# The order of three loads of a unit: first half of K, V, second half of K becomes first half, second half, V

## The chip, the cores and the metric

The kernel runs on one core of a Trainium2 chip. The metric is the device time of one execution in microseconds (us). The times quoted are medians. Single runs of the same kernel lie within about 0.5% of their median for the kernel before. A run counts as slow when it is over 1.5% above the fastest run of the same kernel; only fast runs are compared, and where a slow one plays a part the text says so.

## The reference, cut to what matters

```python
B, Sq, D = 8, 32, 1024
Hq, Hkv, Sk, Dh = 32, 4, 8192, 128
W = min(4096, max(256, Sk // 4))               # 2048
rep = Hq // Hkv                                # 8
q = (x @ wq).reshape(B, Sq, Hq, Dh).transpose(0, 2, 1, 3)
k = repeat(k_cache[:, :, Sk - W:, :], rep, axis=1)
v = repeat(v_cache[:, :, Sk - W:, :], rep, axis=1)
scores = einsum("bhqd,bhkd->bhqk", q, k) * Dh ** -0.5
o = einsum("bhqk,bhkd->bhqd", softmax(scores), v)
return o.transpose(0, 2, 1, 3).reshape(B, Sq, Hq * Dh) @ wo
```

All is bf16. A pair of batch and K/V head is called a **unit**. There are 8 x 4 = 32 units, and each has 2048 rows of K and of V, 512 KB each.

## The kernel before

TensorE makes the scores of a unit (128 keys by 256 queries at a time), ScalarE takes their exponential, and TensorE multiplies the result with V. For the scores, K has to be turned, and there are three ways of it: units 0, 1 and 2 (`PE_T`) are turned by TensorE, eleven units (`V_T`: 4, 7, 9, 12, 14, 17, 19, 22, 24, 27, 29) by VectorE and GpSimd, and the other 18 are turned by the load itself, in two halves of 256 KB. This text calls those halves **a** and **b**. All loads of this phase are issued by one engine, SyncE, one after the other, in program order.

```python
def load_k(self, ui, part=None):
    ...                                         # V_T and PE_T: a plain load into k_raw
    else:
        H = KT // 2
        nc.sync.dma_start_transpose(out=self.kT[ui][:, part * H:(part + 1) * H, :],
                                    in_=src.rearrange("(p j) d -> p (j d)", j=KT)[:, part * H * P:(part + 1) * H * P])

def load_v(self, ui, eng):
    self.v_sb[ui] = self.vp.tile([self.P, self.KT, self.Dh], BF16, name="v_sb", tag="v")
    n = self.KT // (2 if ui >= V_HALVES else 1)
    for j in range(0, self.KT, n):
        eng.dma_start(out=self.v_sb[ui][:, j:j + n, :], in_=...)      # 512 KB, packets of 4096 bytes

def load_unit(self, ui):
    if ui < len(self.units):
        if ui not in V_T:
            self.load_k(ui, None if ui in PE_T else 0)
        self.load_v(ui, self.nc.sync)
        if ui not in V_T and ui not in PE_T:
            self.load_k(ui, 1)
    ...                                         # then plain loads: k_raw of a later unit, pieces of wq and wo

def va_copy(self, ui):                          # V into a padded tile, by VectorE
    out, in_ = self.va[ui % 3][:, :, 0:self.Dh], self.v_sb[ui][:, :, :]
    ...

# in the main loop: 4 slots a unit; the loads of unit u are issued at slot 4 * (u - 5)
loads = {8: [4, 5, 6, 7], **{4 * (u - 5): [u] for u in range(8, len(self.units))}}
```

## Time and profile before

| | kernel before |
|---|---|
| time, median of 3 runs | 183.69 us (183.51 to 184.1) |
| span of the profiled execution | 182.0 us |
| TensorE busy | 98% |
| last load of K, V or weights has landed | 164.0 us |
| bytes moved | 51.72 MB |
| a 512 KB V load, from issue to landing (median) | 7.0 us |
| stretches over 0.3 us in which TensorE does nothing, after 4.5 us | none |

How to read it: TensorE never waits, so it sets the time. But the DMA engines are busy until 164 us as well, and the loads run only a little ahead of TensorE.

### The profile page before, as it was taken

To read this page: it belongs to the slowest core of one execution; us is meant where nothing else is said; L and a number is where in the kernel's file an instruction comes from. 1 tells how busy PE (TensorE), PEld (TensorE's weight loads), DVE (VectorE), ACT (ScalarE), POOL (GpSimd) and SP (SyncE) were. 2 spreads that over 40 slices of the span, in tenths; PEclk is the share of its full clock that TensorE was granted. 3 is DMA by queue.
4 is the path that set the end of the run, shared out by engine and by line. 5 is a ranking of instruction groups with operands and counts; after the bars stand their busy time and mean duration, and the time that the engine had idled before them with its cause. 6 is when DMAs were issued, how large, how long until landed. Compare 5 with 4: busy or idle time off the path is not lost.

```text
span 182.0 us, 5032 instructions
## 1 busy us (share of the span) xinstructions
PE 178.3 (98%) x2041; PEld 152.7 (84%) x2041; DVE 125.3 (69%) x256; ACT 136.3 (75%) x147; POOL 89.5 (49%) x139
## 2 busy tenths in 40 slices
PE   7999999999999999999999999999999999999994
PEld 2999999999999999988787899988787788888853
DVE  0228897699977687679599765697478997354253
ACT  2218898897897888997878787887877788888800
POOL 2004691399918749449686097395078396000000
PEclk9999999999999999999999999999999999999999
DMA  4999999999999999999999999999999999990003
GB/s 177 385 407 405 258 386 321 197 351 195 318 391 251 356 275 325 351 315 362 247 395 257 374 388 249 360 308 286 387 254 286 344 248 388 231 214 0 0 32 91
DMA packets 52953, 51.72 MB, mean 284 GB/s; under 512 B 39744, under 2 KB 40256, under 8 KB 52928
## 3 DMA queue, kind: packets, MB, share of 16 engines
q1 hardware_dynamic: 52352, 50.90, 99.0%
q10 hardware_dynamic: 576, 0.49, 0.8%
q8 instruction: 15, 0.25, 0.5%
q14 instruction: 10, 0.08, 0.1%
HBM read 41.42 MB, written 0.52 MB: 230 GB/s over the span
## 4 chain that ended last, share of the span: by engine, by line
PE 96%; DMA 2%; DVE 0%; issue 0%
PE o_ps L517 32%; PE s_ps L506 31%; PE op_ps L321 15%; PE q_ps L284 12%; PE q_ps L404 3%; DMA x_sb<-in_x_dram 2%; PE xT_ps L380 1%; PE ql_ps L300 1%; PE tp L244 1%; PE kf_ps L396 0%; DVE o_t L331 0%; PE cnt_ps L572 0%
## 5 line engine op out<-in xcount | busy, mean ns | idle before, releaser
L508 ACT ACTIVATE pT<-s_ps 128x1024 bf16<-128x1024 f32 x128 | 128.4, 1027 | 26.7 <-PE s_ps L506 26.4
L269 POOL TENSOR_SCALAR kTv<-kb 32x512 bf16<-32x512 bf16 x127 | 84.7, 667 | 48.8 <-DVE kb L259 27.3
L517 PE MATMUL o_ps<-va,pT 128*128 128x129 bf16 x1024 | 78.8, 220 | 0.0
L517 PEld LDWEIGHTS <-pT 128*128 128x128 bf16 x1024 | 68.5, 98 | 3.2
L506 PE MATMUL s_ps<-QT,kT 128*128 128x256 bf16 x336 | 50.2, 272 | 0.0
L506 PEld LDWEIGHTS <-kT 128*128 128x128 bf16 x336 | 31.9, 98 | 9.4
L321 PE MATMUL op_ps<-wo_sb,OT 128*128 128x512 bf16 (+2 forms) x144 | 36.0, 355 | 0.0
L438 DVE COPY va<-v_sb 128x2048 bf16<-128x2048 bf16 x30 | 25.4, 847 | 7.5 <-DMA v_sb<-in_v_cache_dram 7.1
L259 DVE STREAM_TRANSPOSE kb<-k_raw 128x512 bf16<-128x512 bf16 x44 | 29.5, 687 | 0.6 <-DMA k_raw<-in_k_cache_dram 0.3
L284 PE MATMUL q_ps<-xT,wq_sb 128*128 128x256 bf16 x192 | 28.3, 273 | 0.0
L506 PE MATMUL s_ps<-QT,kTv 128*128 128x256 bf16 x176 | 26.4, 272 | 0.0
L267 DVE COPY kTv<-kb 32x512 bf16<-32x512 bf16 x49 | 22.4, 456 | 1.2
L506 PEld LDWEIGHTS <-kTv 128*128 128x128 bf16 x176 | 17.0, 98 | 6.1
L444 DVE RECIPROCAL RL_all<-o_ps 128x2 f32<-128x2 f32 x32 | 5.3, 165 | 23.6 <-PE o_ps L517 23.3
L284 PEld LDWEIGHTS <-wq_sb 128*128 128x128 bf16 x192 | 16.9, 98 | 1.1
L450 DVE STREAM_TRANSPOSE OT<-o_sb 128x256 bf16<-128x256 bf16 x32 | 14.3, 445 | 1.1
L448 DVE TENSOR_TENSOR o_sb<-o_ps,RL_all 128x256 bf16<-128x256 f32 x32 | 13.6, 424 | 1.1
L321 PEld LDWEIGHTS <-OT 128*128 128x128 bf16 x144 | 11.4, 98 | 2.3 <-DVE OT L450 0.2
L436 POOL TENSOR_SCALAR va<-v_sb 128x2048 bf16<-128x2048 bf16 x2 | 3.8, 1897 | 14.2 <-DMA v_sb<-in_v_cache_dram 14.1
L287 ACT CAST QT<-q_ps 128x512 bf16<-128x512 f32 x12 | 7.0, 583 | 0.2 <-PE q_ps L284 0.2
L328 DVE TENSOR_TENSOR oacc<-op_ps,oacc 128x512 f32<-128x512 f32 x8 | 5.3, 662 | 2.5 <-PE op_ps L321 2.5
L404 PE MATMUL q_ps<-xT,wq_sb 128*128 128x256 bf16 (+1 forms) x64 | 6.0, 246 | 0.0
(35 smaller groups left out, 44.8 us busy)
## 6 DMA issues: line engine op xcount, KB each, us to landing
v_sb<-in_v_cache_dram SPq DMA_DIRECT2D x30, 512.0 KB, 7.0
wo_sb<-in_wo_dram SPq DMA_DIRECT2D x16, 512.0 KB, 6.7
wq_sb<-in_wq_dram SPq DMA_DIRECT2D x13, 512.0 KB, 6.6
k_raw<-in_k_cache_dram SPq DMA_DIRECT2D x13, 512.0 KB, 5.9
wq_sb<-in_wq_dram SPq DMA_DIRECT2D x6, 256.0 KB, 4.8
v_sb<-in_v_cache_dram SPq DMA_DIRECT2D x4, 256.0 KB, 5.1
kT<-in_k_cache_dram SPq DMA_TRANSPOSE x36, 7.3
k_raw<-in_k_cache_dram SPq DMA_DIRECT2D x2, 256.0 KB, 6.2
```

The source lines that it names most:

```text
L259: nc.vector.transpose(out=st["kb"][:, :, sl], in_=self.k_raw[ui][:, :, sl])
L267: nc.vector.tensor_copy(out=out, in_=in_)
L269: nc.gpsimd.tensor_scalar(out=out, in0=in_, scalar1=1.0, scalar2=1.0, op0=ALU.mult, op1=ALU.mult)
L284: nc.tensor.matmul(st[k][:, hl % 2, :], lhsT=self.wq_t[g, i][:, c % (DC // 2), hl * P:(hl + 1) * P], rhs=self.xT[:, c, :], start=(c == 0 a ...
L321: nc.tensor.matmul(ps[:, 0:w], lhsT=self.OT[:, gq, c, t * P:(t + 1) * P], rhs=self.wo_t[gq][:, c, n0:n0 + w], start=(k == 0), stop=(k == 7))
L404: nc.tensor.matmul(ps, lhsT=self.wq_t[0, c // H][:, c % H, h * P:(h + 1) * P], rhs=self.xT[:, c, 0:n], start=(c == 0 and h in (0, 2, 4)), ...
L438: self.nc.vector.tensor_copy(out=out, in_=in_)
L448: nc.vector.tensor_tensor(out=o_sb[:, :, :, :], in0=o_ps[:, :, 0:Dh].rearrange("p q (i c) -> p q c i", c=4), in1=rl[:, ui * QT_N:(ui + 1) ...
L450: nc.vector.transpose(out=self.OT[:, g * QT_N:(g + 1) * QT_N, :, b * self.Sq:(b + 1) * self.Sq], in_=o_sb[:, :, :, :])
L506: nc.tensor.matmul(s_ps[:, jj, :], lhsT=self.kT[ui][:, c * CJ + jj, :], rhs=q_u, start=True, stop=True)
L508: nc.scalar.activation(out=pT[:, :, :], in_=s_ps[:, :, :], func=ACT.Exp, bias=0.0, scale=self.scale)
L517: nc.tensor.matmul(o_ps[:, qt, 0:self.VW], lhsT=pT[:, jj, qt * P:(qt + 1) * P], rhs=va[:, j, 0:self.VW], start=(j == 0 and qt == 0), stop= ...
```

## The change

Its intent is to have the whole of K there earlier. V is needed later than K, so it is put behind both halves.

```diff
         if ui < len(self.units):
             if ui not in V_T:
                 self.load_k(ui, None if ui in PE_T else 0)
+                if ui not in PE_T:
+                    self.load_k(ui, 1)
             self.load_v(ui, self.nc.sync)
-            if ui not in V_T and ui not in PE_T:
-                self.load_k(ui, 1)
```

In 18 units the order a, V, b becomes a, b, V. The programs of TensorE, VectorE, ScalarE and GpSimd are the same, instruction by instruction; only SyncE's order differs.

## The prediction

> **What bounds the kernel now.** I read the page of the profile first: part 1 (busy shares), part 2 (slices), part 4 (the chain that ended last).
>
> ```profile
> PE 178.3 (98%) x2041; PEld 152.7 (84%) x2041; DVE 125.3 (69%) x256; ACT 136.3 (75%) x147; POOL 89.5 (49%) x139
> PE   7999999999999999999999999999999999999994
> DMA  4999999999999999999999999999999999990003
> PE 96%; DMA 2%; DVE 0%; issue 0%
> ```
>
> TensorE is busy for 178.3 of 182.0 us, and the chain is TensorE in 96% of the span; its only long DMA piece is the load of x at the start. The next view is the list of waits, for TensorE alone and then for VectorE:
>
> ```profile
> PE warm_ps L372 <- PEq L680: 0.8, 1, 0.8
> PE xT_ps L380 <- DMA x_sb<-in_x_dram: 0.2, 1, 0.2
> ...
> DVE RL_all L444 <- PE o_ps L517: 23.3, 20, 3.2
> DVE va L438 <- DMA v_sb<-in_v_cache_dram: 7.1, 8, 1.9
> ```
>
> The first two lines are all that TensorE ever waits for over 0.15 us. From the starts of single matmuls in the trace: after 4.5 us no two follow each other by more than 0.3 us. So TensorE never waits for a K or a V now. The last line is the only place where a load of the kind that is moved stops an engine: VectorE stands 7.1 us in all before the copy of V into the padded tile.
>
> But the slices show a second resource that is full: the DMA engines are busy in 9 or more tenths until slice 36, about 164 us. Whether the loads arrive in time is therefore a matter of a microsecond. I lined up the landing of each load with the first instruction that needs it. Unit 11 is the tightest:
>
> ```profile
> 58.96 1.42 SPq L200 DMA_TRANSPOSE kT<-in_k_cache_dram  x1
> 60.48 0.52 SPq L208 DMA_DIRECT2D v_sb<-in_v_cache_dram  x1
> 61.05 1.61 SPq L200 DMA_TRANSPOSE kT<-in_k_cache_dram  x1
> ...
> 65.58 0.60 PE L506 MATMUL s_ps<-QT,kT 128*128 128x256 bf16 x4
> 66.31 0.69 DVE L438 COPY va<-v_sb 128x2048 bf16<-128x2048 bf16 x1
> 68.23 0.56 PE L517 MATMUL o_ps<-va,pT 128*128 128x129 bf16 x7
> ```
>
> The columns are start and duration. The first half of K, V and the second half of K land at 65.14, 66.28 and 67.19 us (issue plus the time to landing of each). The scores of unit 11 start at 65.58, 0.44 us after the first half; the second half is needed at 67.80, 0.61 us after it landed; the V copy starts 0.03 us after V landed, and the product with V, which needs the copy, starts at 68.23.
>
> **How a transposing load behaves.** The third thing I looked at is the DMA rate by the microsecond around unit 10's first half (the last two columns are the DMA share and GB/s):
>
> ```profile
> 55.00:56.00 1.00, 1.00 (x14) 0.91 (x12) 0.55 (x2) 0.80 (x1) 0.94 (x2) 1.00 1.05 389
> 56.00:57.00 1.00, 1.00 (x16) 0.93 (x13) 1.00 (x2) 0.90 (x1) 0.94 (x2) 1.00 2.71 239
> 57.00:58.00 1.00, 1.00 (x16) 0.94 (x14) 0.39 (x2) 0.70 (x2) 0.88 (x3) 1.00 0.19 30
> 58.00:59.00 1.00, 1.00 (x16) 0.94 (x14) 0.94 (x3) 0.70 (x2) 0.94 (x2) 1.00 1.15 321
> q8 instruction: 15, 0.25, 0.5%
> ```
>
> Transfers nearly stop for a microsecond. By the records of single packets, a half of K takes 0.94 us when undisturbed, and 2.3 to 2.5 us in about 16 of 36 cases, always standing still in its middle: here 22 of its packets hang from 56.7 to 58.15 us, while one or two engines still work off 2048-byte packets of the load before. Those engines are late because an instruction fetch (last line above) of 16 KB took one of them for about 1 us. The fetches start at 22.7, 33.9, 41.0, 52.9, 63.1, 74.2, 83.8, 97.2, 108.5, 117.5, 129.8, 143.4, 154.3 us; the next transpose after each one is a slow one (5a, 5b, 8a, 10a, 11b, 15a, 16a, 18b, 20b, 23a, 25a, 28a, 30a, where a and b are the halves). The others are clean. So the stall goes with the fetch, not with the neighbours of the transpose: about 1.4 us for each fetch, whatever the order.
>
> **What the Trainium skill says.** "DMA: Bandwidth & Descriptors", section "Queues, rings and completion order": each DMA engine takes turns between the queues that have work for it. This agrees with one engine falling behind by a fetch. "Runtime: NRT & Kernel Launch", section "Instruction fetch mechanics": instructions come in blocks of 16 KiB, 256 instructions. TensorE's 2041 matmuls and 2041 weight loads make 4082 / 256 = 16 blocks, and the page counts 15 such packets in the span; the change adds no instruction, so the number stays. "Advanced Engine Details and Errata", section "X-Bar Transpose (TRN2)", has transposes as fast as regular loads. The trace disagrees: 256 KB in 0.94 us is 279 GB/s, beside 389 GB/s in the row 55:56 of plain loads. The order doesn't change that either. No page that I read prices two transposes in a row against two with a load between.
>
> **The change, part by part.** It adds and removes nothing: 18 units (3, 5, 6, 8, 10, 11, 13, 15, 16, 18, 20, 21, 23, 25, 26, 28, 30, 31) issue a, b, V in place of a, V, b.
> 1. The first half stays where it is: 0 us.
> 2. The second half no longer has V ahead of it. A 512 KB load takes 1.25 us in the trace, so b lands about 1.25 us sooner. TensorE did not wait for it: 0 us gained.
> 3. V has one half more ahead of it: 0.94 us later, so it lands about where b landed before. VectorE stands in its V copy until then. The sum over the units of (old landing of b minus old start of the V copy), where positive, is 0.8+0.3+0.8+0.9+1.5+0.3+0.7+0.9+0.9+0.8+0.1+1.9 = 9.9 us for units 5, 6, 10, 11, 13, 15, 16, 18, 20, 21, 23, 26. VectorE's wait for V goes from 7.1 to about 17 us. It has 182.0 - 125.3 = 57 us idle, so it catches up in each unit.
> 4. Does this reach TensorE? Margin = first product with V minus (old landing of b plus the copy): unit 11: 68.23 - 67.19 - 0.69 = 0.35 us; unit 5: 38.48 - 37.26 - 0.81 = 0.4; unit 16: 92.66 - 91.48 - 0.77 = 0.4; unit 26: 146.90 - 145.46 - 0.65 = 0.8; all others 0.9 or more. All positive, so 0 us; I allow 0.2 us for the units under 0.5.
> 5. VectorE's blocks that follow the V copy (K turned in 32x32 blocks for the 11 other units) end 1.4 us or more ahead of their scores; a delay of 0.8 to 1.9 us within them is mostly absorbed, but unit 4 and 7 (1.4 and 1.8) lie before most of the delay. 0 us.
>
> Sum: 0 to +0.2 us on 183.69.
>
> **Rivals.**
> - *Two transposes in a row disturb each other, or leave the queue empty.* For: the issue of b is held up until half of a is through (in unit 10 it ends at 58.24 us, a's data at 58.69), so today V's 1.25 us cover what b still needs. After the change nothing covers it. Against: the halves 30b and 31a already lie next to each other in the queue; 31a's first packet came at 158.93, 30b's last at 158.94, both took 0.94 us. If each of 18 pairs lost 0.25 us, unit 16, the ninth, would be 2.2 us late against a margin of 0.4, and unit 26, the fifteenth, 3.7 against 0.8: 3 us, 186.6.
> - *A stall in both halves of each pair*: 18 more of 1.4 us are 25 us of loads, against about 6 us of lead at the last unit: over 195 us. Only if I misread the fetches.
> - *The change takes the stalls away or lets loads run further ahead.* Then all lands sooner, and TensorE, already without waits, ends when it did: 183.7. There is no way to 2% faster, as the matmuls alone fill 98%.
> - *VectorE is held too long and TensorE waits for its blocks or for a free output bank*: some tenths, 184.5.
>
> **Range and chances.** The middle is 183.9: 183.69 plus the 0.2 of step 4. Runs of before spread over 0.6 us. The low end is 183.2, only scatter. The high end, 185.2, holds half of the first rival. Beyond 2% (187.4) lie the second rival and a large form of the first: 4%. Faster by 2% would need 180.0, under the present busy time plus the start: 1%.
>
> **What would show it.** TensorE's waits stay as in the fence above, the chain stays 96% TensorE (steps 2, 4). VectorE's wait for V rises to 12 to 20 us (step 3). The loads still end near 164 us, and slow halves stay 14 to 18 of 36, each the first after a fetch (the stall). Wrong: waits of TensorE for the V copy or for K in the waits or the chain; halves of K slow without a fetch before them; a gap between a and b or between b and V; a later end of the loads.

## The result, and the profile after

The changed kernel takes 190.45 us (190.08 to 191.57, 4 runs), the kernel before 183.89 us (183.51 to 184.2, 4 runs) in the same rounds. The ratio is 1.037, with a 95% interval of 1.032 to 1.042. A ratio is always the mean time of one kernel's fast runs over that of the other's of the same rounds, so it is not quite the ratio of the medians that are quoted. The change makes the kernel 3.7% slower; the prediction of "no change" was wrong.

The page of the changed kernel (busy time of the engines; busy tenths of TensorE and of the DMA engines in 40 slices of the span; the chain of work that ended last):

```profile
PE 180.0 (95%) x2041; PEld 151.8 (80%) x2041; DVE 123.0 (65%) x256; ACT 136.4 (72%) x147; POOL 87.9 (47%) x139
PE   7999999999999979999898999999999988999994
DMA  6999999999999999999999999999999999992003
PE 60%; DMA 19%; DVE 10%; SPq 8%; issue 1%; DVEq 0%
```

TensorE's work has hardly grown (178.3 to 180.0 us), yet the span has (182.0 to 188.7). The first line alone says that TensorE now stands idle. The slices say where: TensorE falls under 9 tenths for the first time in the 15th slice, which begins at 66 us (14 x 188.7 / 40), and again and again after it. In the chain TensorE's share falls from 96% to 60%, and in its place come loads, VectorE, and "SPq", which is SyncE itself. The DMA engines are busy one slice longer: the last load lands at 172.0 us instead of 164.0, though the bytes are the same.

The list of waits of the changed kernel (engine, line, what it waited for: total us, times, longest):

```profile
DVE va L438 <- DMA v_sb<-in_v_cache_dram: 28.1, 16, 4.0
...
PE o_ps L517 <- DVE va L438: 3.9, 7, 0.8
...
PE s_ps L506 <- DMA kT<-in_k_cache_dram: 0.5, 2, 0.4
```

VectorE's wait for V grows from 7.1 to 28.1 us. TensorE's product with V (L517), which waited for nothing before, now waits for VectorE's copy of V. The list names 3.9 us of it; by the gaps of over 0.3 us between TensorE's matmuls in the trace it is more, some 5.9 us ahead of products with V and 1.1 us ahead of scores. Compared with the kernel before, instruction by instruction, TensorE is 1.9 us late at unit 11, 3.9 at unit 16, 5.0 at unit 21, 5.9 at unit 26 and 6.7 from unit 27 on. That is the whole difference of the spans.

Why does V come so late? The chain of the changed kernel around unit 16 (start us, duration us, what) answers it:

```profile
87.88 0.28 SPq L200
88.17 0.04 issue
88.21 3.53 SPq L200
91.74 0.05 issue
91.79 0.02 SPq L208
91.81 0.04 issue
91.84 3.89 DMA v_sb<-in_v_cache_dram
95.73 0.02 issue
95.76 0.73 DVE va L438
```

Read it from below. The copy of V waits for the load of V, which is issued at 91.84. It could not be issued sooner, because for 3.5 us SyncE sits in L200, the transposing load of b. Issuing b takes SyncE several microseconds, and SyncE issues in order.

The same three loads as SyncE issued them (start us, duration of the issue us, engine, line; a and b of the changed kernel stand in one row). First the kernel before, then the kernel after:

```profile
82.36 1.23 SPq L200 DMA_TRANSPOSE kT<-in_k_cache_dram  x1
83.69 1.39 SPq L208 DMA_DIRECT2D v_sb<-in_v_cache_dram  x1
85.14 3.11 SPq L200 DMA_TRANSPOSE kT<-in_k_cache_dram  x1
88.30 0.57 SPq L168 DMA_DIRECT2D wq_sb<-in_wq_dram  x1
```

```profile
86.27 5.46 SPq L200 DMA_TRANSPOSE kT<-in_k_cache_dram  x2
91.84 0.52 SPq L208 DMA_DIRECT2D v_sb<-in_v_cache_dram  x1
```

In both kernels the issue of this b is held for 3 us and more. By the records of single packets, it ends 0.43 to 0.68 us before the last data of a have landed in 17 of the 18 units of the changed kernel, and 0.43 to 0.48 us in 14 units of the kernel before: that is when about half of a has moved. What differs is what lies between a and b. Before, V's 1.25 us of data come in between, so SyncE is free again 2.58 us before b's data end (88.30 against 90.88 us) and the load behind b is issued in time. After, nothing lies in between, and SyncE is free only 1.36 us before b's data end (91.84 against 93.20). I call this time, from the start of the next load's issue to the end of b's data, the **lead**. It is 1.36 to 1.50 us in ten units of the changed kernel.

What such a lead does to the DMA engines is in the rate per half microsecond (the last two columns are the DMA share and GB/s), first before, where b of unit 16 ends at 90.88, then after, where it ends at 93.20:

```profile
90.50:91.00 0.50, 0.50 (x6) 0.26 (x4) 0.25 (x1) 0.50 (x1) 0.46 (x1) 1.00 1.25 332
91.00:91.50 0.50, 0.50 (x8) 0.46 (x6) 0.50 (x1) 0.30 (x1) 0.46 (x1) 1.00 1.05 406
91.50:92.00 0.50, 0.50 (x9) 0.39 (x7) 0.47 (x2) 0.40 (x1) 0.48 (x1) 1.00 1.06 389
```

```profile
93.00:93.50 0.50, 0.50 (x9) 0.47 (x8) 0.14 (x1) 0.00 (x0) 0.21 (x1) 1.00 1.25 148
93.50:94.00 0.50, 0.50 (x9) 0.38 (x7) 0.00 (x0) 0.47 (x1) 0.44 (x2) 1.00 0.62 147
94.00:94.50 0.50, 0.50 (x6) 0.35 (x5) 0.00 (x0) 0.50 (x1) 0.50 (x1) 1.00 0.97 360
```

Before, the rate goes on at about 400 GB/s behind b. After, it is under 150 for a microsecond: the transfers run nearly dry, because V was issued too late to flow when b ended.

I measured this for every unit: the time from b's last packet until 128 KB behind it have landed, less the 0.33 us that 128 KB take at 389 GB/s, with negative values as zero. I call it the **dry time**. Unit 31, the last of the loads, is left out. Over the 17 other units it sums to 1.4 us before and 6.4 us after, 0.38 us a unit. It is 0.45 to 0.80 us in the ten units with a lead of 1.36 to 1.50 us (3, 6, 10, 11, 13, 15, 16, 21, 25, 28). It is nothing in units 5, 18, 20, 26 and 30, whose b is slowed by an instruction fetch and lasts long enough for a lead of 2.7 us or more.

The chain from cause to effect, as far as the trace suggests it, is then: b's issue blocks SyncE; V is issued late; the transfers run dry for half a microsecond in ten units; the loads slip, by 8 us in all until their end; and when their small head start is used up, at about unit 11, TensorE waits. The added dry time (6.4 less 1.4 us) covers 5.0 of the 8 us. Where the other 3 us come from is not shown.

### The profile page after: what moved, and what is told of

Same layout as the page of the kernel before. It is cut to its first block, busy times and chain, and to the rows that moved or that the text cites. A ratio compares the mean times of both kernels' runs of the same rounds, so it can differ in the third digit from the quotient of the medians.

```text
span 188.7 us, 5031 instructions
## 1 busy us (share of the span) xinstructions
PE 180.0 (95%) x2041; PEld 151.8 (80%) x2041; DVE 123.0 (65%) x256; ACT 136.4 (72%) x147; POOL 87.9 (47%) x139
## 4 chain that ended last, share of the span: by engine, by line
PE 60%; DMA 19%; DVE 10%; SPq 8%; issue 1%; DVEq 0%
PE o_ps L517 21%; PE s_ps L506 18%; DMA v_sb<-in_v_cache_dram 16%; PE op_ps L321 10%; PE q_ps L284 7%; SPq L200 7%; DVE va L438 4%; DMA wq_sb<-in_wq_dram 3%; DVE kb L259 2%; PE q_ps L404 1%; DVE kTv L267 1%; PE tp L244 1%; DVE o_sb L448 1%; SPq L168 1%; PE ql_ps L300 1%
## 5 line engine op out<-in xcount | busy, mean ns | idle before, releaser
L269 POOL TENSOR_SCALAR kTv<-kb 32x512 bf16<-32x512 bf16 x127 | 83.0, 654 | 55.8 <-DVE kb L259 40.4
L517 PE MATMUL o_ps<-va,pT 128*128 128x129 bf16 x1024 | 78.7, 220 | 4.0 <-DVE va L438 3.9
L517 PEld LDWEIGHTS <-pT 128*128 128x128 bf16 x1024 | 68.4, 98 | 8.7 <-issue 5.6
L438 DVE COPY va<-v_sb 128x2048 bf16<-128x2048 bf16 x30 | 24.4, 813 | 28.3 <-DMA v_sb<-in_v_cache_dram 28.1
L267 DVE COPY kTv<-kb 32x512 bf16<-32x512 bf16 x49 | 21.7, 442 | 1.2
```

Source lines behind the costliest of these rows:

```text
L267: nc.vector.tensor_copy(out=out, in_=in_)
L269: nc.gpsimd.tensor_scalar(out=out, in0=in_, scalar1=1.0, scalar2=1.0, op0=ALU.mult, op1=ALU.mult)
L438: self.nc.vector.tensor_copy(out=out, in_=in_)
L517: nc.tensor.matmul(o_ps[:, qt, 0:self.VW], lhsT=pT[:, jj, qt * P:(qt + 1) * P], rhs=va[:, j, 0:self.VW], start=(j == 0 and qt == 0), stop= ...
```

## The experiments

The experiments had two theories to separate. **Theory 1:** the dry moments are what costs the time, whichever load falls behind the pair. **Theory 2:** it is V's later place in the queue, by 0.94 us and more, whatever the queue does. A third idea (**Theory 3** in the expectations), that two adjacent transposes slow each other, is not borne out by the trace: there is no gap between a and b (-0.02 us), and the data of the 36 halves flow for 58.6 us in all, against 59.8 before. 18 of the 36 are slow (over 1.5 us) against 17 before. In each kernel 15 of them are the first behind an instruction fetch, or one runs beside them. For the rest (18a, 30a and 31b; in the kernel before 26a and 31b) no fetch begins until their last quarter of a microsecond, if at all, and what slows them is not known.

All runs passed the record's check of the result, even e7 and e8, which are wrong by design; so this check doesn't see their error. "Loads end" is the last landing of a load of K, V or weights. Times before are of the same rounds.

| run | order | us | before | ratio | loads end | dry time |
|---|---|---|---|---|---|---|
| (after) | a, b, V | 190.45 | 183.89 | 1.037 | 172.0 | 6.4 |
| e1_v_first | V, a, b | 192.44 | 184.34 | 1.045 | 173.7 | 6.3 |
| e2_other_between | a, other, b, V | 188.04 | 184.34 | 1.023 | 165.9 | 2.6 |
| e4_half_v_between | a, half V, b, half V | 189.58 | 184.34 | 1.030 | 171.0 | 1.2 |
| e3_v_act_queue | V by ScalarE | 218.47 | 184.34 | 1.188 | - | - |
| e5_v_around_b | V's partitions 0 to 63 before b, 64 to 127 after | 196.99 | 184.22 | 1.070 | 179.5 | 1.3 |
| e6_v_split_before | both before b (control) | 198.0 | 184.22 | 1.075 | 182.1 | 0.5 |
| e7_fewer_loads_after | a, b, V; 12 loads fewer | 186.75 | 184.22 | 1.016 | - | 8.9 |
| e8_fewer_loads_before | a, V, b; 12 loads fewer | 186.54 | 184.22 | 1.012 | - | 1.0 |
| e10_sync_held_1 | a, V, b, hold | 184.57 | 183.79 | 1.006 | 166.0 | 1.8 |
| e9_sync_held_2 | a, V, b, hold x2 | 190.48, one fast run | 183.79 | none | 179.3 | 8.4, slow run |
| e11_sync_held_4 | a, V, b, hold x4 | 205.55 | 183.79 | 1.116 | 191.9 | 16.4 |
| e12_held_in_ten | a, V, b, hold x2 in ten units | 190.38 | 184.21 | 1.034 | 172.6 | 5.9 |

The dry times of this table are the ones defined above. The expectations were written with a slightly different count, so their sums differ by some tenths; and they count the lead from the end of the next load's issue (2.0 and 0.85 us), not from its start (2.58 and 1.36).

### V ahead of both halves

```diff
         if ui < len(self.units):
+            self.load_v(ui, self.nc.sync)
             if ui not in V_T:
                 self.load_k(ui, None if ui in PE_T else 0)
-            self.load_v(ui, self.nc.sync)
-            if ui not in V_T and ui not in PE_T:
-                self.load_k(ui, 1)
+                if ui not in PE_T:
+                    self.load_k(ui, 1)
```

> V goes ahead of the two adjacent halves (V, a, b). Theory 1 (SyncE issues in order; b's issue is held until half of a is through, so the load behind b is issued too late and the DMA engines run dry for about 0.4 us a unit, 6.6 us over 18 units): the dry moment stays, it only falls on whichever load follows b. Loads end at 169 to 172 us, the first 32 large packets after b take 0.8 to 1.1 us in the units whose b is not slowed by an instruction fetch, and the time is 187 to 190 us, with TensorE waiting for the second half of K instead of V's copy. Theory 2 (only the place of V counts: it lands 0.94 us later and holds VectorE): V is now earlier than in the kernel before, so 183.5 to 184.5 us and loads end near 164. Theory 3 (two transposes in a row disturb each other in the DMA engines): slow halves well above 18 of 36; the trace of the changed kernel already has 18, so I expect 16 to 19.

It took 192.44 us (190.71 to 195.16, one of the four runs slow). Theory 2 falls as the whole cause: V is now earlier in its unit's order than in either kernel, and the kernel is slower still. But K has moved back, so the price of K's place is in this time too. The halves are still next to each other, the dry moments are still there (6.3 us; they fall on whatever load is behind b), and now TensorE waits for K. From its list of waits:

```profile
PE s_ps L506 <- DMA kT<-in_k_cache_dram: 3.9, 3, 2.4
```

The time was 2.4 us above the upper end of my range. The waits before scores are longer here (up to 2.8 us at unit 16), and 20 halves were slow instead of 18; how much each adds I can't tell.

### Another load between the halves

V stays last, as in the changed kernel, but a plain load that the unit issues anyway is put between a and b. Only 14 of the 18 units have one.

```diff
+        raw = [u for u, at in V_T.items() if at[0] == ui]
+        extra = [...]                      # the unit's k_raw, wq and wo loads, in their old order
         if ui < len(self.units):
             if ui not in V_T:
                 self.load_k(ui, None if ui in PE_T else 0)
+                if ui not in PE_T:
+                    if extra:
+                        extra.pop(0)()
+                    self.load_k(ui, 1)
             self.load_v(ui, self.nc.sync)
-            ...                            # second half, k_raw, wq and wo as before
+        for p in extra:
+            p()
```

> a, one other plain load of the same unit (raw K or a weight piece), b, V; in 14 of 18 units there is such a load, in units 6, 21, 30, 31 the order is a, b, V. V still comes after both halves, and even later in the queue. Theory 1: 14 of 18 dry moments go, loads end at 164 to 166.5 us; V lands 2.2 us later than in the kernel before, so TensorE waits about 1 us at the tightest units, and the time is 184 to 186 us. Theory 2 (place of V): V lands later than in the changed kernel relative to its K, so as slow or slower: 190 to 193 us.

It took 188.04 us (187.16 to 188.73). The dry moment goes where the cover was given, as theory 1 has it. Around unit 16, where b ends at 92.63 (DMA share and GB/s last):

```profile
92.40:92.90 0.50, 0.50 (x9) 0.47 (x8) 0.00 (x0) 0.20 (x1) 0.50 (x1) 1.00 1.19 379
92.90:93.40 0.50, 0.50 (x9) 0.38 (x7) 0.00 (x0) 0.50 (x1) 0.44 (x2) 1.00 1.09 442
```

In the 14 covered units the dry time is 0 to 0.12 us; in units 6 and 21, which have no other load to put in, it stays at 0.93 and 0.67, and in unit 30, which has none either, it is 0.38. The loads end at 165.9 us, 6 us earlier than in the changed kernel. But the time was 2 us above what I expected. V now has b and a whole 512 KB load ahead of it, and the product with V waits for it in the early units, where the loads have no head start yet. All of TensorE's 3.3 us of delay are there by unit 17:

```profile
PE o_ps L515 <- DVE va L436: 2.8, 4, 1.4
```

So the dry moments explain most of the slip at the end of the loads (6 of 8 us go with them), and V's place has a price of its own when V goes far enough back.

### V issued by ScalarE

```diff
-            self.load_v(ui, self.nc.sync)
-            if ui not in V_T and ui not in PE_T:
-                self.load_k(ui, 1)
+                if ui not in PE_T:
+                    self.load_k(ui, 1)
+            self.load_v(ui, self.nc.sync if ui in V_T or ui in PE_T else self.nc.scalar)
```

> a, b on SyncE as in the changed kernel, V of the 18 units issued by ScalarE on its own queue, so V's issue isn't held behind b's. Theory 1: no dry moment behind b, as V waits ready in the other queue: loads end at 162 to 166 us, time 183.5 to 186 us (ScalarE gives some 0.4 us of issuing for each of 18 V, which may show). Theory 3 (adjacent transposes disturb each other): loads end near 171 us as in the changed kernel, time 189 to 191.

It took 218.47 us, and tells nothing on the question. The loads wait on ScalarE for free buffers, and that holds its exponentials: TensorE waited 17.8 us for them. TensorE's granted clock was also lower, 0.93 to 0.95 beside 1.0 in the kernel before. The idea was that V should not stand behind b in SyncE's order; it moved the block to an engine that has work to do.

### Half of V between the halves

```diff
+                self.load_k(ui, 0)
+                self.load_v(ui, self.nc.sync, 0)     # first half of every row, packets of 2048 bytes
                 self.load_k(ui, 1)
+                self.load_v(ui, self.nc.sync, 1)
```

> a, first half of V, b, second half of V: half of the cover that the kernel before has (0.63 us of load in place of 1.25). Theory 1: what is left of the dry moment is 0.6 us shorter, 0 to 0.25 us a unit, loads end at 163.5 to 167.5 us, time 184 to 187 us. Theory 2 (V complete only after b): V is complete where it is in the changed kernel, so 189 to 191 us.

It took 189.58 us. The lead is 1.94 to 2.13 us in ten units, and the dry time 1.2 us, as theory 1 expected. But the loads still ended at 171.0 us, and the time is the one that theory 2 had forecast (189 to 191), not that of theory 1 (184 to 187). The edit has side effects: the packets are half as long (2048 bytes), there are 18 more issues, and 21 halves are slow. I did not separate them, so this run supports the link between lead and dry time, and speaks against the dry time as the only cause of the loss.

### V split by partitions, around b or ahead of it

Here the packets stay at 4096 bytes, and a control has the same split without the late piece.

```diff
+                self.load_k(ui, 0)
+                self.load_v(ui, self.nc.sync, 0)     # partitions 0 to 63
                 self.load_k(ui, 1)                   # control e6: this line comes last
+                self.load_v(ui, self.nc.sync, 1)     # partitions 64 to 127
```

> a, V of partitions 0 to 63, b, V of partitions 64 to 127; packets stay 4096 bytes, unlike in the run with halves of V by columns. V is complete after b, as in the changed kernel, but 0.63 us of load stand between a and b. Theory 1 (dry moment behind b): it shrinks by 0.63 us, from 0.5 to 0.8 us to 0 to 0.2 us in the units whose b isn't slowed; loads end at 164 to 167 us; time 184.5 to 187 us, the rest being V's later landing. Theory 2 (only V's later landing counts): V is complete as late as in the changed kernel, 189 to 191 us with loads ending near 165.

> Control for the run before it: a, V of partitions 0 to 63, V of partitions 64 to 127, b, so the order of the kernel before with V in two instructions. If the splitting itself costs nothing: 183.5 to 184.7 us, loads end at 163 to 165 us. If it costs, the difference of these two runs, not the time of the other, is what V's place costs.

They took 196.99 us (196.78 to 197.25) and 198.0 us (197.36 to 198.54). Both are far above the ranges that I gave. The split itself costs 13.8 us, by the control: a 4096-byte packet takes 197 (e5) and 207 ns (e6) on average instead of 172, a b that isn't slowed takes 1.23 to 1.28 us instead of 0.94, and the loads end at 179.5 us or later. TensorE waits for loads, or for the copies of V behind them, throughout both kernels (11 us by their lists of waits). What can be read is the comparison of the two: with V complete only behind b, the kernel is 0.5% faster than with b last. So in this kernel, which its loads bind, V complete behind b is not slower than b last, as long as something covers b's issue. For the kernel of the change, which has a head start to lose, this is a hint and no more.

### The changed order with fewer loads

If the dry moments cost time because the loads have no head start, then more head start should hide them. Here the weights wq of the first group are used for all four groups, so 12 loads of 512 KB go. The result is wrong.

```diff
         def piece(i, n):
+            if g > 0:
+                self.wq_t[g, half] = self.wq_t[0, half]
+                return
...
-        self.wp = pool("wp", 6, long_ctx)
+        self.wp = pool("wp", 4, long_ctx)
```

e7 has this and the change, e8 has this and the old order.

> Wrong result on purpose: the changed kernel with the weights of the first group used for all groups, so 12 loads of 512 KB, some 15.6 us of the DMA engines' time, are not made. Theory 1 (loads lag, TensorE waits for V's copy only because there is no lead): loads run ahead, TensorE hardly waits, time 183.3 to 185 us though the dry moments behind b are still there. A theory in which the order costs TensorE or VectorE something by itself, whatever the lead: 188 us or more.

> Control for the run before it, wrong result on purpose: the kernel before with the same 12 loads left out. TensorE bound: 183.3 to 184.5 us, within 1 us of the run before it by theory 1.

They took 186.75 us (186.44 to 187.41) and 186.54 us (185.59 to 186.9), both above the ranges that I gave. The dry moments of e7 are all there, 8.9 us against 1.0. But up to unit 24 TensorE is only 0.13 us later than in the kernel before, where the changed kernel is 5.04 us late. What TensorE waits for in e7, then in e8:

```profile
PE o_ps L520 <- DVE va L441: 1.2, 2, 0.7
```

```profile
PE s_ps L509 <- DMA kT<-in_k_cache_dram: 1.2, 1, 1.2
```

Both lose about 2 us at the end, after 140 us. The DMA engines had stood idle for 12 and 20 us around 120 to 140 us, which I put down to the smaller pool of weight buffers in this edit. The difference of the two is 0.2 us. So up to unit 24, where the loads are ahead, the same dry moments cost nothing.

### SyncE held behind b, in the old order

The last test leaves the order a, V, b alone and makes only the late issue: behind each b, SyncE loads a register from memory n times (a zero), which holds it before the next load.

```diff
                 self.load_k(ui, 1)
+                for _ in range(n):
+                    self.nc.values_load(self.zero[0:1, 0:1], engines=[SP], min_val=0, max_val=1)
```

> The kernel before, order a, V, b untouched, but SyncE is kept busy once after each b (a register load of a zero, some 0.5 to 0.7 us). In the kernel before the load behind b has been issued 2.0 us before b's end, in the changed kernel 0.85 us. Theory 1 (a late issue behind b is what costs): 1.4 us ahead of b's end, nearly enough, dry moment 0 to 0.3 us a unit: loads end at 163.5 to 168 us, 183.8 to 187 us. Theory 2 (V's place): V is where it was, 183.5 to 184.7.

> The same with two such register loads, so the load behind b is issued some 0.6 to 1.0 us before b's end, as late as in the changed kernel. Theory 1: dry moments of 0.4 to 0.8 us come back though the order is that of the kernel before, loads end at 169 to 173 us, 187 to 192 us. Theory 2 (V's place): 183.5 to 184.7.

> The same with four, so the load behind b is issued some 0.4 us after b's end. Theory 1: about 1.7 us dry in each of 18 units, less the units with an instruction fetch: 20 to 30 us more than the kernel before at the end of the loads, 200 to 215 us. Theory 2: 183.5 to 185.

One register load leaves a lead of 1.5 to 2.3 us in eleven units, and costs 0.6% (184.57 us, 183.63 to 185.79). That is within the 2% that count as the same, and both theories had room for it. Four leave a lead between -0.2 and 1.9 us in all units but one, and cost 11.6% (205.55 us, 204.3 to 206.24), with a granted clock of 0.975 to 0.992 beside 1.0. The run with two counted as slow in three of four executions (190.48 us in the single fast one); it stands between the others, and I draw nothing else from it. With four, the dry moment behind b of unit 16, which ends at 101.55, is longer than any of the change:

```profile
101.50:102.00 0.50, 0.50 (x10) 0.48 (x8) 0.47 (x2) 0.20 (x2) 0.50 (x1) 1.00 0.10 15
102.00:102.50 0.50, 0.50 (x8) 0.33 (x5) 0.50 (x1) 0.50 (x1) 0.37 (x1) 1.00 0.97 45
102.50:103.00 0.50, 0.50 (x7) 0.40 (x5) 0.47 (x2) 0.46 (x1) 0.00 (x0) 1.00 0.33 70
```

Across these kernels lead and dry time add up to 1.7 to 2.1 us in most units: a lead of -0.2 us leaves 2.0 us dry, 0.3 us leaves 1.5, 0.8 us leaves 1.1, 1.4 us leaves 0.6, and from 2.5 us on nothing is left. By this measure, the data of a load behind a transpose flow in full about 2 us after its issue starts.

The last run holds SyncE with two register loads, but only in the ten units in which the change had a short lead:

```diff
+                for _ in range(2 if ui in (3, 6, 10, 11, 13, 15, 16, 21, 25, 28) else 0):
+                    self.nc.values_load(...)
```

> The run with two register loads fell mostly into slow runs, so once more with the two register loads only in the ten units in which the changed kernel ran dry (3, 6, 10, 11, 13, 15, 16, 21, 25, 28); the order is that of the kernel before. Theory 1, dry moments alone suffice: 4 to 7 us dry in all, loads land until 168 to 172 us, 186.5 to 191 us, with TensorE waiting for K. If V's later landing is needed for the loss: under 185.5 us with the same dry moments.

It took 190.38 us (188.77 to 191.0, five fast runs), ratio 1.034 (1.031 to 1.037), beside 1.037 of the change. The dry time is 5.9 us (6.4 in the change), and the loads end at 172.6 us (172.0). The lead became 0.9 to 1.5 us in seven of the ten units; in 6, 11 and 21 it stayed over 2 us. Of the 5.9 us, 0.66 fall in unit 26, whose lead is 3.7 us; this I can't explain, as little as the 0.68 us of unit 23 in the kernel before. Around unit 16, the load behind b is issued at 91.81, 1.30 us before b's data end at 93.12, and the rate falls as it did in the change:

```profile
91.81 0.39 SPq L170 DMA_DIRECT2D wq_sb<-in_wq_dram  x1
93.00:93.50 0.50, 0.50 (x5) 0.36 (x4) 0.50 (x1) 0.50 (x1) 0.42 (x2) 1.00 1.17 121
93.50:94.00 0.50, 0.50 (x10) 0.48 (x9) 0.47 (x2) 0.20 (x2) 0.50 (x1) 1.00 0.91 156
```

Here V lies where it always lay, and b is last as before, so TensorE waits for K:

```profile
PE s_ps L510 <- DMA kT<-in_k_cache_dram: 3.8, 4, 1.9
```

So a late issue by itself, with nothing reordered, is enough for a slip of the loads and a loss of this size. How it gets there is not in all parts the way of the change: the data of the 36 halves flow for 63.0 us here (58.6 in the change), and 4 of TensorE's 4.9 us of delay in the profiled execution arise at units 6 and 21. There 6b and 21a are slow with no fetch before them, and 6b and 21b are reported landed 2.0 us after their last data (0.5 us in unit 16), a fetch having begun just then. So where the fetches fall has a part in this run's time. The change makes TensorE wait for V and this run makes it wait for K: in each it waits for the load that is last in the unit.

No variant is faster than the kernel before, in which TensorE is busy 98% of the span.

## Why the prediction was wrong

- **What bounds the kernel** was read rightly: TensorE, with the loads a microsecond behind as a second limit. The tightest margin in the text, 0.35 us at unit 11, is where TensorE's first large delay fell (1.3 us); up to unit 10 it was under 1 us late in all.
- **The stall with the fetch** held for most: 18 slow halves of 36, 15 of them with a fetch. "The others are clean" was a misreading: besides the 13 named, 3a, 13a, 26a and 31b were slow in the kernel before, the last two with no fetch before them. The second rival (18 more stalls) was rightly dropped, and so was the hope for a gain.
- **Step 1 and 2** (a stays, b lands 1.25 us sooner, nothing gained) held only at first. b follows a without a gap, and up to unit 10 it landed 0.3 to 1.0 us sooner. From unit 11 on it landed later than before, by 5.8 us at unit 31, and a by 8.4.
- **Step 3 failed.** It priced V's delay as one half of K, 0.94 us, "so it lands about where b landed before". V lands 0.4 us later than that in unit 5, 1.7 in unit 10, 2.4 in unit 13, 4.3 in unit 16, 6.7 in unit 21 and 8.0 in unit 31. The delay is not one fixed step for each unit; it adds up, and the dry moments, which push back all that follows, cover most of it. VectorE's wait for V, predicted 12 to 20 us, was 28.1.
- **The root is the dismissal of the first rival**, "Two transposes in a row disturb each other, or leave the queue empty". The "for" said the right thing: the issue of b is held, V's 1.25 us cover it, and after the change nothing does. The "against" looked at halves 30b and 31a, adjacent and without a gap. That pair answers whether the second transpose is disturbed. It says nothing on the load *behind* the second transpose, which is the one that the held issue makes late. The evidence answered half of the rival, and the whole of it was put aside.
- **The rival's own sum** was near in kind. It took 0.25 us for each of 18 pairs and came to 186.6. Measured are 0.38 us a unit, which is less in some and 0.45 to 0.80 in ten. It also charged the excess over the margin at two units; the measured delay went on growing to 6.7 us at unit 27.
- **Step 4** (all margins positive, so 0 us) was sound for a shift of 0.94 us and wrong for one that grows to 8 us. One margin was misread: unit 13 had 0.68 us, not "0.9 or more"; it played no part.

What stays open: how the 6.6 us divide between the dry moments and V's later place. The old order with the late issue alone has a ratio of 1.034. With little dry time, V last has 1.023 and half of V behind b has 1.030, so taking the dry moments away won back less than half of the time. V split around b has 0.995 against its control. The parts don't add up; that they overlap, because each uses the same small head start, is my reading and was not tested.

## What to carry to other kernels

When one engine issues loads in order, look at which issues hold it, and compare the start of the next issue with the end of the data ahead of it. Here a lead of about 2 us kept the transfers going, and a long plain load between two transposing ones is what gave it; it is a cover for the second one's issue, and moving it away is a cost that no count of bytes shows. If the loads are nearly as long as the bound engine's work, half a microsecond of dry time a unit adds up until it is on the path; where they ran ahead, the same dry time cost nothing here.

## What the Trainium skill lacked or had wrong

- No page that I read says that issuing a second transposing load holds the issuing engine until about half of the one ahead has moved (2.6 to 7.6 us for b in 17 units of the changed kernel, ending 0.43 to 0.68 us before the data of the first end), so that the load behind is issued late. In ten units the transfers ran dry for 0.45 to 0.80 us behind it; a late issue alone cost 3.4% (e12).
- "DMA: Bandwidth & Descriptors", section "Latency and other measured facts", gives about 0.6 us to the first byte of a load issued from SyncE. This is the first byte alone: where the load behind b was issued less than 0.5 us before b's end (e11), its first packets started 0.7 to 1.0 us after its issue began in six units, 0.3 to 0.4 us of it the issue itself. What the page lacks is the time until the data flow in full behind a transposing load, 1.7 to 2.1 us here.
- The same page, section "Rules for kernel authors", says of two transfers to disjoint halves of the partitions that they only serialize and are not worth it. Here the split of V into two such halves, in the old order (e6), cost 13.8 us over 18 units, with packets of 4096 bytes at 207 ns instead of 172. The page gives no such price.
- "Advanced Engine Details and Errata", section "X-Bar Transpose (TRN2)": this section has transposing loads as fast as regular ones. Here a half of K that nothing slowed took 0.94 us, 279 GB/s, beside 389 GB/s for plain loads; and 17 to 18 of the 36 halves took 1.6 to 3.6 us, most of them at an instruction fetch.
